# A Mamba-2 scan followed by a GELU network: one filler matmul moved in, one pad taken out, and three state decays given to ScalarE

## The chip, the core and the metric

The kernel runs on one core of a Trainium2 chip. The metric is the device time of one execution in microseconds (us); lower is better. A core has five engines that run side by side, each through its own list of instructions in order: TensorE (PE; its weight loads are listed apart as PEld), VectorE (DVE), ScalarE (ACT), GpSimd (POOL) and SyncE (SP, here only for starting transfers). They wait for one another through semaphores. Matmuls write into PSUM, a small memory of eight banks; everything else lies in SBUF.

## What is computed

Two stages, the second on the output of the first. The first is a state-space scan over 4 batches, 8 heads, 768 steps, with values of width 32 and a state of 16 x 32 for each head:

```python
for c in range(nc):                      # chunks of 32 steps
    cum = np.cumsum(log_a[:, :, sl], axis=-1)
    L = np.exp(cum[..., :, None] - cum[..., None, :]) * causal
    CB = np.einsum('bhin,bhjn->bhij', Cc, Bc)
    y_intra = np.einsum('bhij,bhjd->bhid', CB * L, xc)
    y_inter = np.einsum('bhin,bhnd->bhid', Cc, state) * np.exp(cum)[..., None]
    y[:, :, sl] = y_intra + y_inter
    Bx = np.einsum('bhjn,bhjd->bhjnd', Bc, xc) * decay_from_j
    state = decay_full * state + np.sum(Bx, axis=2)
```

The second takes the 3072 rows of 256 values: `h = x @ w_in` (256 x 2048), `g = h * sigmoid(1.702 h)`, `out = g @ w_out` (2048 x 256).

## The kernel before

The 3072 rows are six groups (g = 0 to 5), each of one chunk of 128 steps of all four batches, 512 rows. A group's scan is done in two pairs of batches; `pairs` names the two pairs of a group, PG and PG + 1 being those of group 1. A chunk is cut into two sides of 64 steps.

**Scan of one group.** `score` multiplies C with B (L626) into an area of PSUM, four banks that exist once (the pool `psa`, tag "cb"). `weigh` (L637, VectorE) multiplies the decays L with those scores, one call for each pair. `gain` (L657, TensorE) computes what each side adds to the state. `keep(g, i)` makes the state after side i: `decayed` (L675) multiplies the state before with the decay over the side into a tile "old" (L679, VectorE, one buffer), and two instructions (L696) add the gain. `carry_first` does the same for the second side of group 0: one product L679 and one sum (L997, by `plus`). `finish` has two steps: `inter` (L738) multiplies the states with C, `intra` (L751) multiplies the weighed L with x; both add into the area of PSUM that the scores were in, and ScalarE copies the sums to yT (L785). Group 0 is different: `early` in `intra` means that its sums lie in four banks of their own, that each bank is copied when it is done (L763), and that `dense`, a matmul of ones with ones whose result nobody reads (L440), stands ahead of the products of the first pair. `pads` are the same in small: 32 x 4 outputs (L436).

**The network.** For group 0, `hidden` (L812) multiplies yT with w_in for 16 columns blocks f, ScalarE applies the activation (L816), and `project_all` multiplies with w_out (L910). From group 1 on, products of 2 x 2 blocks are done with seven multiplications instead of eight (L868, L878, L970, and L977 for the last group), from sums that VectorE prepares (`mix_in` L830, `mix_y` and `mix_g` L836, `mix_w` L933).

**The weights** come as 64-bit floats. VectorE and ScalarE put them together as 32-bit floats (L203 to L251), piece by piece, during the start, the hidden layer of group 0 and its projection; `narrow(9)` is the last piece.

**The order** is written out by hand, and `in_order` at the end keeps it on every engine. `at(in_project[0], f, ...)` puts work of group 1's scan into the projection of group 0, ahead of its block f: at 9 the scores, the gains, the states and the weighings, at 13 the first step of `finish` and `mix_in(1)`, at 15 its second step. At the start, one bank area takes the decays of the first pair (masks L522, two `dense`, the pads, then `differ_of` L528, which waits for the cumulative sums of VectorE, L377); the scores of group 0, its `weigh` in halves, `finish(range(PG), (0,))`, `gain`, and `finish(range(PG), (1,))` follow. In the last of these the second pair's products stand for t = 0 first: half k = 0, half k = 1, each of eight matmuls. The trace lists every matmul of 32-bit floats as two records.

Of the kernel before, what the change touches and what calls it, by code (L numbers as in the profile page):

```python
# [11 lines left out]
AF = mybir.ActivationFunctionType  # L12
# [4 lines left out]
P = 128  # L17
# [18 lines left out]
def kernel(  # L36
# [31 lines left out]
    nc = tc.nc  # L68
# [363 lines left out]
    def pads(n, t, start=True):  # L432

        for i in range(n):
            c = 32 * (i % R)
            nc.tensor.matmul(out=t[c:c + 32, :4], lhsT=ones[:32, :32], rhs=ones[:32, :4],  # L436
                             start=start, stop=True, tile_position=(0, c), skip_group_check=True)
# [177 lines left out]
    def score(pairs):  # L615

        cb = area(f"cb{pairs[0]}").rearrange("p r (k e) -> p r k e", k=2 * PG)
        for n, p in enumerate(pairs):
            s = st[p]
            BT, CT = s["BT"], s.pop("CT")  # L620
            s["cb"] = cb[:, :, 2 * n:2 * n + 2]
            for k in range(2):
                for i, side in enumerate(SIDES):
                    for r in range(R):
                        rows = slice(32 * r, 32 * r + 32)
                        nc.tensor.matmul(  # L626
                            out=s["cb"][side, r, k].rearrange("p (q i) -> p q i", q=Q),
                            lhsT=BT[rows, k, side], rhs=CT[rows, k, :, side],
                            start=True, stop=True, tile_position=(32 * r, H * i),
                            skip_group_check=True)  # L630

    def weigh(p, ks=(slice(0, 2),)):

        Lv = Ls[p].rearrange("p k r q i -> p k r (q i)")
        cb = st[p]["cb"].rearrange("p r k e -> p k r e")
        for k in ks:
            nc.vector.tensor_tensor(out=Lv[:, k], in0=Lv[:, k], in1=cb[:, k], op=ALU.mult)  # L637
# [3 lines left out]
    def gain(pairs, sides=range(2)):  # L641

        g = pairs[0] // PG
        sides = [i for i in sides if i == 0 or g < NG - 1]
        for i in sides:
            if g == 0:
                A = area("A0_1")[:, 0] if i else begun_y["banks"][2][:, 2 * P:]
            else:
                A = bank(f"A{g}_{i}")
            increment[g, i] = A[:, :NB * Q * D].rearrange("p (b e) -> p b e", e=Q * D)  # L650
        for p in pairs:
            b = place(p)[1]
            for k in range(2):
                for r in range(R):
                    heads = slice(Q * r, Q * r + Q)
                    for i in sides:
                        nc.tensor.matmul(  # L657
                            out=increment[g, i][32 * r:32 * r + 32, b + k],
                            lhsT=BE[p][0][SIDES[i], k, r],
                            rhs=rx[p][SIDES[i], k, heads].rearrange("p h d -> p (h d)"),  # L660
                            start=True, stop=True, tile_position=(H * i, 32 * r),
                            skip_group_check=True)
# [12 lines left out]
    def decayed(g, i):  # L675

        t = ssd.tile([P, NB, Q * D], FP32, tag="old", name=f"old{g}_{i}", bufs=1)
        e = i * H + H - 1
        nc.vector.tensor_tensor(out=t, in0=state[g][:, 0] if i else state[g - 1][:, 1],  # L679
                                in1=since[g][:, :, e:e + 1].to_broadcast([P, NB, Q * D]),  # L680
                                op=ALU.mult)
        return t
# [17 lines left out]
    def keep_both(g):  # L700
        for i in range(2):
            keep(g, i)

    def finish(pairs, steps=range(2)):


        g, first = divmod(pairs[0], PG)
        early = pairs[0] < PG
        if 0 in steps:
            if early:  # L710
                banks = begun_y["banks"] = [bank(f"y0_{i}") for i in range(4)]
                y = [t[:, :2 * P].rearrange("p (k i) -> p k i", i=H) for t in banks]
                begun_y[0] = [[y[2 * t + i] for t in range(NK)] for i in range(2)], set()
            else:
                both = area(f"y{pairs[0]}")[:, :, :len(pairs) * 2 * H].rearrange(
                    "p (s t) (k i) -> p s t k i", s=2, i=H)
                begun_y[pairs[0]] = [[both[:, i, t] for t in range(NK)] for i in range(2)] + [both], set()
        y, begun = begun_y[pairs[0]]

        def begin(i, t, parts):  # L720
            new = not begun & {(i, t, q) for q in parts}
            begun.update((i, t, q) for q in parts)
            return new

        def inter(n, p, ts=range(2)):

            b = place(p)[1]
            for k in range(2):
                for i in range(2):
                    if g == 0 and i == 0:  # L730
                        continue
                    old = (state[g][:, 0] if i else state[g - 1][:, 1])[:, b + k]
                    for r in range(R):
                        t = r // 2
                        if t not in ts:
                            continue
                        rows, to = slice(32 * r, 32 * r + 32), Q * D * (r % 2)
                        nc.tensor.matmul(  # L738
                            out=y[i][t][to:to + Q * D, 2 * n + k], lhsT=old[rows],
                            rhs=st[p]["CsT"][rows, k, SIDES[i]],  # L740
                            start=begin(i, t, range(Q * (r % 2), Q * (r % 2) + Q)), stop=early,
                            tile_position=(32 * r, to), skip_group_check=True)

        def intra(n, p, ts=range(2)):
            L = Ls[p]
            for k, t in [(k, t) for t in ts for k in range(2)] if early else [
                    (k, t) for k in range(2) for t in ts]:
                for q in range(HB):
                    h = t * HB + q
                    for i, side in enumerate(SIDES):  # L750
                        nc.tensor.matmul(  # L751
                            out=y[i][t][D * q:D * q + D, 2 * n + k], lhsT=rx[p][side, k, h],
                            rhs=L[side, k, h // Q, h % Q],
                            start=begin(i, t, (q,)), stop=not early, tile_position=(H * i, D * q),
                            skip_group_check=True)

        cols = slice(2 * first * P, 2 * (first + len(pairs)) * P)

        if first == 0 and g not in yT:
            yT[g] = ffn.tile([P, NK, TG], FP32, tag="yT", name=f"yT{g}")  # L760
        if early:
            def copied(i, t):
                nc.scalar.activation(  # L763
                    yT[g][:, t, cols].rearrange("p (k s i) -> p s k i", s=2, i=H)[:, i], y[i][t],
                    AF.Copy)

            if 0 in steps:
                for t in range(NK):
                    dense(begun_y["banks"][0][:, 2 * P:])
                    intra(0, pairs[0], (t,))  # L770
                return
            for t in range(NK):
                intra(1, pairs[1], (t,))
                copied(0, t)
                for n, p in enumerate(pairs):
                    inter(n, p, (t,))
                copied(1, t)
        else:
            for step in steps:
                for n, p in enumerate(pairs):  # L780
                    (inter, intra)[step](n, p)
            if 1 not in steps:
                return
            for i in range(2):
                nc.scalar.activation(  # L785
                    yT[g][:, :, cols].rearrange("p t (k s i) -> p s t k i", s=2, i=H)[:, i], y[2][:, i],
                    AF.Copy)
        state.pop(g - 1, None)
        for p in pairs:
            st.pop(p)  # L790
            Ls.pop(p)
# [292 lines left out]
        mask_banks(1, r, seconds[r])  # L1084
    for k in range(2):
        dense(both[:, k, 2 * P:], 4 - k, False)
    pads(17, both[:, 0, 2 * P:], False)
    differ_of(0)
    turn_blocks(0, "C")
    turn_blocks(0, "B")  # L1090
# [66 lines left out]
    def at(places, i, *work):  # L1157
        places.setdefault(i, []).extend(work)
# [12 lines left out]
    for i, k, c in ((2, 1, 1), (3, 2, 2), (4, 4, 4), (5, 6, 8), (6, 9, 12), (7, 12, 15)):  # L1171
# [12 lines left out]
       lambda: ends_turned(PG + 1), lambda: mask_blocks(PG), lambda: mask_blocks(PG + 1),  # L1184
       lambda: clip_rows(1), lambda: decay_rows(1), lambda: since_start(PG, nc.gpsimd),
       lambda: since_start(PG + 1, nc.gpsimd), lambda: narrow(9))
    at(in_project[0], 9, lambda: score(pairs), lambda: gain(pairs), carry_first, lambda: keep_both(1),
       lambda: weigh(PG), lambda: weigh(PG + 1))
    at(in_project[0], 13, lambda: finish(pairs, (0,)))
    at(in_project[0], 15, lambda: finish(pairs, (1,)))  # L1190
    at(in_project[0], 13, lambda: mix_in(1),
# [198 lines left out]
```

## Time and profile before

| what | value |
|---|---|
| median of 3 runs | 349.52 us (349.3 to 349.52) |
| the profiled execution, its own time | 349.2 us |
| its span, first to last instruction | 347.5 us |
| granted TensorE clock | 1.000 |
| DMA | 25.79 MB, mean 74 GB/s |

Every number of the trace below is in us from the start of the span. "Busy" counts an engine's instructions; matmuls overlap in the array, so a record of 0.38 us may be followed by the next 0.22 us later. A text in square brackets, `[0.93 <-DVE L L637]`, gives how long the engine stood idle before the instruction and what released it; "issue" stands for idle time in which the engine waited for nothing that the profile shows. "x16" counts records. Where one line has many forms, times are of one form only.

The page cuts the span into 40 slices of 8.7 us; a digit is a busy share in tenths:

```profile
PE   7999999989999999999999999999999999999996
DVE  7899999999799897839985639985555653555463
ACT  6689664005454324644333543442444322554320
PEclk9999999999999999999999999999999999999999
```

VectorE is as busy as TensorE in the first ten slices, where it puts the weights together and scans, and half idle after the middle. ScalarE stands still in the eighth and ninth slice, during the end of the projection of group 0.

### The profile page before, as it was taken

To read this page: it belongs to the slowest core of one execution; us is meant where nothing else is said; L and a number is where in the kernel's file an instruction comes from. 1 tells how busy PE (TensorE), PEld (TensorE's weight loads), DVE (VectorE), ACT (ScalarE), POOL (GpSimd) and SP (SyncE) were. 2 spreads that over 40 slices of the span, in tenths; PEclk is the share of its full clock that TensorE was granted. 3 is DMA by queue.
4 is the path that set the end of the run, shared out by engine and by line. 5 is a ranking of instruction groups with operands and counts; after the bars stand their busy time and mean duration, and the time that the engine had idled before them with its cause. 6 is when DMAs were issued, how large, how long until landed. Compare 5 with 4: busy or idle time off the path is not lost.

```text
span 347.5 us, 8555 instructions
## 1 busy us (share of the span) xinstructions
PE 340.7 (98%) x3514; PEld 281.0 (81%) x3514; DVE 257.6 (74%) x489; ACT 149.6 (43%) x335; POOL 41.5 (12%) x80
## 2 busy tenths in 40 slices
PE   7999999989999999999999999999999999999996
PEld 5669964545788888888888888888888888899996
DVE  7899999999799897839985639985555653555463
ACT  6689664005454324644333543442444322554320
POOL 8306500300495000000000000000000000000000
PEclk9999999999999999999999999999999999999999
DMA  4799974703638000554122326120000120000221
GB/s 102 226 299 309 273 154 121 131 9 73 109 90 130 2 0 17 92 110 91 29 35 61 47 87 113 24 32 8 2 4 0 20 32 12 0 2 1 32 31 60
DMA packets 82831, 25.79 MB, mean 74 GB/s; under 512 B 68856, under 2 KB 81144, under 8 KB 82792
## 3 DMA queue, kind: packets, MB, share of 16 engines
q1 hardware_dynamic: 79912, 23.19, 31.1%
q0 software_dynamic: 1888, 1.74, 2.3%
q8 instruction: 27, 0.44, 0.6%
q10 hardware_dynamic: 992, 0.33, 0.4%
q14 instruction: 12, 0.10, 0.1%
HBM read 21.99 MB, written 3.24 MB: 73 GB/s over the span
## 4 chain that ended last, share of the span: by engine, by line
PE 80%; DVE 14%; issue 2%; ACT 2%; ACTq 1%; POOL 0%; DVEq 0%
PE acc L970 28%; PE X L868 19%; PE Y L878 14%; PE acc L977 7%; DVE p L245 3%; PE y L751 2%; PE h L812 2%; PE y L738 2%; PE o L910 2%; DVE m L231 2%; DVE p L203 1%; PE cb L626 1%; DVE m L206 1%; DVE w_in L251 1%; DVE L L637 1%
## 5 line engine op out<-in xcount | busy, mean ns | idle before, releaser
L873 ACT ACTIVATE ac<-X 128x256 f32<-128x256 f32 x76 | 29.1, 383 | 79.7 <-PE X L868 79.3
L970 PE MATMUL acc<-mg,mw 128*128 128x256 f32 x192 | 54.5, 379 | 0.0
L997 DVE TENSOR_TENSOR gT<-Y,ac 128x512 f32<-128x512 f32 x38 | 26.2, 690 | 37.0 <-PE Y L878 33.6
L845 ACT ACTIVATE gT<-gT 128x512 f32<-128x512 f32 (+1 forms) x76 | 39.3, 519 | 31.7 <-DVE gT L997 31.0
L868 PE MATMUL X<-my,mi 128*128 128x256 f32 x152 | 45.1, 379 | 0.0
L997 DVE TENSOR_TENSOR gT<-Y,b 128x256 f32<-128x256 f32 x38 | 15.8, 419 | 34.4 <-PE Y L878 34.4
L970 PEld LDWEIGHTS acc<-mg,mw 128*128 128x128 f32 x192 | 36.5, 190 | 5.0
L812 PE MATMUL h<-yT,w_in 128*128 128x128 f32 (+2 forms) x206 | 36.2, 335 | 0.0
L970 PE MATMUL acc<-gT,w_out 128*128 128x256 f32 x128 | 35.5, 379 | 0.0
L812 PEld LDWEIGHTS h<-yT,w_in 128*128 128x128 f32 x206 | 27.8, 191 | 7.4 <-issue 5.6
L868 PEld LDWEIGHTS X<-my,mi 128*128 128x128 f32 x152 | 28.0, 190 | 3.8
L910 PE MATMUL o<-gT,w_out 128*128 128x512 f32 x64 | 28.6, 597 | 0.0
L836 DVE TENSOR_TENSOR mg<-gT 128x512 f32<-128x512 f32 x40 | 27.2, 681 | 0.0
L970 PEld LDWEIGHTS acc<-gT,w_out 128*128 128x128 f32 x128 | 24.2, 190 | 3.4 <-ACT yT L785 0.2
L873 ACT ACTIVATE b<-X 128x256 f32<-128x256 f32 x38 | 14.6, 384 | 20.6 <-PE X L868 20.2
L868 PE MATMUL X<-yT,w_in 128*128 128x256 f32 x76 | 23.2, 389 | 0.0
L878 PE MATMUL Y<-yT,w_in 128*128 128x256 f32 x76 | 22.7, 381 | 0.0
L878 PE MATMUL Y<-my,mi 128*128 128x256 f32 x76 | 22.6, 379 | 0.0
L868 PE MATMUL X<-my,w_in 128*128 128x256 f32 x76 | 22.6, 381 | 0.0
L878 PE MATMUL Y<-yT,mi 128*128 128x256 f32 x76 | 22.4, 379 | 0.0
L910 PEld LDWEIGHTS o<-gT,w_out 128*128 128x128 f32 x64 | 11.8, 190 | 13.2 <-issue 12.7
L1029 POOL DMA_DIRECT2D out_dram<-ob x32 | 17.3, 550 | 26.3 <-DVE ob L1024 26.1
(146 smaller groups left out, 574.5 us busy)
## 6 DMA issues: line engine op xcount, KB each, us to landing
a<-scratch SPq DMA_DIRECT2D x18, 256.0 KB
bits<-in_moe_w_out_dram SPq DMA_DIRECT2D x8, 512.0 KB
x<-in_x_dram SPq DMA_DIRECT2D x20, 128.0 KB
bits<-in_moe_w_in_dram SPq DMA_DIRECT2D x8, 256.0 KB
bits<-in_moe_w_in_dram SPq DMA_DIRECT2D x4, 512.0 KB
out_dram<-ob SPq DMA_DIRECT2D x128, 16.0 KB
af<-in_a_dram SPq DMA_DIRECT2D x20, 64.0 KB
zC<-in_C_dram SPq DMA_DIRECT2D x36, 32.0 KB
```

The source lines that it names most:

```text
L245: nc.vector.scalar_tensor_tensor(out=p2[:, cols], in0=low[:, cols], scalar=0x80000000, in1=p2[:, cols], op0=ALU.bitwise_and, op1=ALU.bitwi ...
L812: nc.tensor.matmul(out=h[:, cols], lhsT=w_in[:, f, k], rhs=yT[g][:, k, cols], start=(k == 0 and e == 0), stop=(k == NK - 1), skip_group_ch ...
L836: nc.vector.tensor_tensor(out=t[:, 0:2], in0=B[:, :, 1], in1=B[:, 0], op=ALU.subtract)
L845: nc.scalar.activation(o, i, AF.Silu, scale=GELU_SCALE)
L868: nc.tensor.matmul(out=s["X"], lhsT=lhsT, rhs=rhs, start=i == "1", stop=i == "4", skip_group_check=True)
L873: nc.scalar.activation(copy, s["X"], AF.Copy)
L878: nc.tensor.matmul(out=o, lhsT=lhsT, rhs=rhs, start=s.pop("new", False), stop=i != "5", skip_group_check=True)
L910: nc.tensor.matmul(out=o[c], lhsT=w_out[:, c, f], rhs=gT[g, f // 2][:, f % 2], start=(f == 0), stop=(f == NF - 1), skip_group_check=True)
L970: nc.tensor.matmul(out=acc[g][0][i], lhsT=w, rhs=h, start=(j == 0 and (i, 0) in begins), stop=(j == NF // 2 - 1), skip_group_check=True)
L977: nc.tensor.matmul(out=o[k] if type(o) is list else o[:, cols], lhsT=h[:, cols], rhs=w, start=(j == 0 and (i, k) in begins), stop=(j == NF ...
L997: nc.vector.tensor_tensor(out=o, in0=v, in1=w, op=ALU.add)
L1029: (nc.sync if g else nc.gpsimd).dma_start(out=rows[:, b, :, cols], in_=t[32 * r:32 * r + 32, b * P:(b + 1) * P].rearrange("p (u e) -> p u ...
```

## The change

Three things. `decayed` does the product for g below 2 on ScalarE, as four copies with a scale, one for each batch (128 x 64 each), instead of one instruction of VectorE (128 x 256). `keep_both(1)`, which stood ahead of both weighings of group 1, becomes two calls, one after each weighing. In `intra` of group 0, for the second pair and t = 0, one `dense` is put between its halves k = 0 and k = 1, and the pads at the start become 16 instead of 17.

```diff
@@ decayed
         t = ssd.tile([P, NB, Q * D], FP32, tag="old", name=f"old{g}_{i}", bufs=1)
         e = i * H + H - 1
+        if g < 2:
+            for b in range(NB):
+                nc.scalar.activation(t[:, b], (state[g][:, 0] if i else state[g - 1][:, 1])[:, b],
+                                     AF.Copy, scale=since[g][:, b, e:e + 1])
+            return t
         nc.vector.tensor_tensor(out=t, in0=state[g][:, 0] if i else state[g - 1][:, 1],
                                 in1=since[g][:, :, e:e + 1].to_broadcast([P, NB, Q * D]),
                                 op=ALU.mult)
@@ intra
             for k, t in [(k, t) for t in ts for k in range(2)] if early else [
                     (k, t) for k in range(2) for t in ts]:
+                if early and n and not t and k:
+                    dense(begun_y["banks"][0][:, 2 * P:])
                 for q in range(HB):
@@ the start
     for k in range(2):
         dense(both[:, k, 2 * P:], 4 - k, False)
-    pads(17, both[:, 0, 2 * P:], False)
+    pads(16, both[:, 0, 2 * P:], False)
     differ_of(0)
@@ the order within the projection of group 0
-    at(in_project[0], 9, lambda: score(pairs), lambda: gain(pairs), carry_first, lambda: keep_both(1),
-       lambda: weigh(PG), lambda: weigh(PG + 1))
+    at(in_project[0], 9, lambda: score(pairs), lambda: gain(pairs), carry_first, lambda: weigh(PG),
+       lambda: keep(1, 0), lambda: weigh(PG + 1), lambda: keep(1, 1))
```

## The prediction

> **What bounds the kernel now.** I read the busy shares first, then who waited for whom on TensorE, then the order of time around the longest wait, then the same at the second place that the change touches.
>
> ```profile
> PE 340.7 (98%) x3514; PEld 281.0 (81%) x3514; DVE 257.6 (74%) x489; ACT 149.6 (43%) x335; POOL 41.5 (12%) x80
> ...
> PE ab L528 <- DVE cum L377: 1.0, 1, 1.0
> PE y L738 <- DVE L L637: 0.9, 1, 0.9
> PE busy L447 <- PEq L1374: 0.9, 1, 0.9
> PE y L751 <- issue: 0.5, 1, 0.5
> ```
>
> TensorE is busy 98% of the span, and its whole list of waits has four entries, 3.3 us together. Whoever removes one of them, without adding TensorE work, moves everything behind it; whoever shortens work on another engine anywhere else gains nothing. Two of the four, y L738 and y L751, lie where the change works. In order of time the first is this:
>
> ```profile
> 64.02 7.13 PE L910 MATMUL o<-gT,w_out 128*128 128x512 f32 x16
> 66.45 0.41 DVE L679 TENSOR_TENSOR old<-S,L 128x256 f32<-128x256 f32 x1
> 66.90 0.42 DVE L997 TENSOR_TENSOR S<-S,old 128x256 f32<-128x256 f32 x1
> 67.36 0.42 DVE L679 TENSOR_TENSOR old<-S,since 128x256 f32<-128x256 f32 x1
> 67.90 0.61 DVE L696 SCALAR_TENSOR_TENSOR S<-A,part,old 128x128 f32<-128x128 f32 x2
> 68.55 0.42 DVE L679 TENSOR_TENSOR old<-S,since 128x256 f32<-128x256 f32 x1
> 69.07 0.61 DVE L696 SCALAR_TENSOR_TENSOR S<-A,part,old 128x128 f32<-128x128 f32 x2
> 69.60 2.34 DVE L637 TENSOR_TENSOR L<-L,cb 128x1024 f32<-128x1024 f32 x2
> 72.09 1.29 PE L738 MATMUL y<-CsT,S 32*64 32x64 f32 x64 [0.93 <-DVE L L637]
> 76.94 1.48 PE L751 MATMUL y<-L,x 64*32 64x64 f32 x128
> 78.46 1.09 ACT L785 ACTIVATE yT<-y 128x512 f32<-128x512 f32 x2 [20.54 <-PE y L751]
> ```
>
> Columns: start, length, engine, line, operation, count. VectorE goes through eight steps without a pause (carry_first, keep, keep, weigh, weigh), and TensorE, done with the projection at 71.15, stands until the second weighing ends at 71.94: finish writes its sums into the PSUM area that the weighings read. ScalarE has nothing from 57.92 to 78.46. At the other place, early in the kernel:
>
> ```profile
> 11.78 0.70 PE L440 MATMUL y<-ones 128*128 128x256 f32 x2
> 12.41 0.45 PE L751 MATMUL y<-L,x 64*32 64x64 f32 x32
> ...
> 13.60 0.17 PEld L751 LDWEIGHTS y<-L,x 64*32 64x32 f32 x10 [0.25 <-DVE bits L170]
> 14.44 0.31 PE L751 MATMUL y<-L,x 64*32 64x64 f32 x7 [0.52 <-issue]
> ```
>
> The weight loads of the first half of the second rows (k = 0) end at 13.35; the second half starts at 13.60, after its weighing ended at 13.55, does nine records, and pauses from 13.92 to 14.44 for nothing that the profile names, before the last seven.
>
> **The change, part by part.** *(a) States.* VectorE loses the three old products (L679), and one keep moves behind the second weighing. What is left ahead of finish, with start-to-start times of the rows above: the sum of carry_first 0.46 (66.90 to 67.36), a weighing 1.13 (half of 69.60 to 71.86), one keep of two instructions 0.65 (67.90 to 68.55), the last weighing 1.22 (the median of L637). From 66.45, where the weight join before it lets go, that ends at 66.45 + 0.46 + 1.13 + 0.65 + 1.22 = 69.91; with the 0.15 between the end of the weighing (71.94) and TensorE's start (72.09), TensorE could go at 70.06.
>
> *(b) ScalarE* gets three groups of four copies, 128x64 each, a shape that the trace doesn't have. Nearest rows: the copies of L396 (128x128) come 0.29 apart, those of L603 (128x256) 0.40 apart with a mean of 0.494. From 0.29 and 0.40 the line goes to 0.24 at 64 columns; above, 0.494 each with no overlap. I take 0.25, since fewer columns must lie at the low end. Group one, for carry_first, has its inputs (S0, the first group's decays) long before, and runs in ScalarE's gap from 57.92. Group two needs the sum of carry_first, which ends at 66.87: four copies end at 67.87 (by 0.25) or 68.85 (by 0.494). VectorE comes for them at 66.45 + 0.46 + 1.13 = 68.04, so it waits 0 to 0.81, and finish may go at 70.06 to 70.87. Group three uses the same buffer as group two: it waits for the keep that reads it (about 68.7), ends about 69.7 (70.7 by the high price), and the last keep follows the second weighing. Behind it on VectorE stand mix_in and the transposes, at about 70.5 instead of 71.86. Queued behind the copies on ScalarE is only L785 at 78.46.
>
> *(c) What TensorE gets.* Its work ahead of finish is unchanged: it arrives when its own queue lets it. Where it doesn't stall, the next matmul starts 0.07 before the modelled end of the one before (76.94 against 77.01 for L751), so 71.08. Both ends of (b) lie before that. L738 starts at 71.08 instead of 72.09: **1.01 us gained**, for 0.93 by the list of waits alone. Where L738 doesn't stall (91.41) its 64 records take 1.16 and not 1.29, so up to 0.13 more; I leave that to the range. Only 1.01 of VectorE's 2.03 (72.09 - 70.06) counts.
>
> *(d) Where the stall could go next.* Behind it TensorE has no wait to the end, and VectorE runs ahead: y copies end 0.6 before hidden at 80.17, the second group's weighings at 89.15 against L738 at 91.41. All these are released by TensorE or by VectorE, which come forward by 1.01 and about 1.3. The loads that meet them: x for the next gain, issued at 77.83 when L751 frees its buffer, moves along, and with a landing of at most 4.2 (this tensor's loads through POOL) is there at 82.0 for a gain at 83.70; the spread for the scan at 79.75 was issued from 66.35, and no transfer is busy from 70 to 72. I cost it at nothing.
>
> *(e) Filler and pad.* The filler is one full matmul, two records, like L440 at 11.78: 0.63 until the next L751 starts. It stands between k = 0 and k = 1, so it can begin at 13.35 and delays k = 1 from 13.60 to 13.98, or at the worst, begun only at 13.60, to 14.23. Nine records later (0.17 of weight loads) come 14.15 to 14.40, still inside the pause that ends at 14.44. I cost it at 0: its cover is 0.25 of waiting for VectorE and 0.52 of pause. If the pause is not tied to the clock but to the instruction, it moves along, and the filler costs 0.38, at most 0.63, straight on the path into hidden (16.28). The pad: 34 records in 0.47, so 0.03 less, ahead of a wait of 1.00 for VectorE (6.00): nothing.
>
> The trace's instruction queue q8 moved 27 packets, 0.44 MB, one of them at 11.6, another at 16.9, none from 13.8 to 14.6. The Trainium skill (Runtime: NRT & Kernel Launch, Instruction fetch mechanics) says that an engine's program is streamed in 16 KiB blocks of 256 instructions, fetched ahead, and that crossing a block is mostly hidden; 0.44 MB in 27 packets agrees with the size, and by that rule a pad less and a filler more leave every block boundary behind the filler at the same instruction, so the pause stays before the same seven records. By the words "mostly hidden" the pause would be no crossing at all, and the sum is the same.
>
> *Sum:* -1.01 + 0 + 0 = -1.01 on a profiled execution of 349.2 (span 347.5, and 1.7 around it), which is 0.32 under the median of 349.52. Taken off the median: **348.5**.
>
> **The rivals.**
>
> 1. *The filler is not hidden.* For it: a full matmul holds off the small ones (0.63 at 11.78), and nothing names what ends the pause. Against: the pause lies right behind it and is longer than 0.38. Time: 349.52 - 1.01 + 0.38 = 348.9, to 349.1 with 0.63.
>
> 2. *ScalarE becomes the last.* It decides when the four copies take more than 71.08 - 0.15 - 1.22 - 0.65 - 66.87 = 2.19, or 0.55 each. At 0.7 each finish goes at 66.87 + 2.8 + 0.65 + 1.22 + 0.15 = 71.69, a gain of 0.40: 349.1. Against: copies of four times the size (L603) have a mean of 0.494.
>
> 3. *The microsecond is given back* at a later wait (a load with a fixed time of issue): 349.5. Against: (d).
>
> 4. *Slower: the clock.* The pads stand in TensorE's 1.00 of idling before 6.00. If one fewer let the granted clock fall there, the decay products L528, 2.63 on the chain of waits from 6.00 to 8.63, would take up to twice as long: 349.52 - 1.01 + 2.63 = 351.1; it decides from 1.01 of loss on. Against: the granted clock is 1.000, every slice has a 9, and the pad is 0.03 of work.
>
> The Trainium skill (TensorE: Matmul & The Clock Gate, Part 1: The HAM clock gate) says that the clock halves after an idle window of about 3.4 us that runs free of the kernel, not after short gaps. The 1.00 us gap at full clock agrees; by that rule 4 costs nothing.
>
> **How the numbers follow.** A measurement of this kernel can tell about 0.2%, 0.70 us, from no change: faster means under 348.82. The forecast, 0.60, with its own range 348.2 (the 0.13 more and the spread of 0.2 between runs) to 348.8. Rival 1: 0.20, of which 0.06 falls under 348.82. Rival 2: 0.05. Rival 3: 0.07, of which 0.02 ends over 350.2. Rival 4: 0.08. Faster 0.66, within 0.23 (0.14 + 0.05 + 0.05, rounded down), slower 0.11 (0.02 + 0.08, rounded up). The range goes from 348.2 to 349.5: it takes in both ends of rivals 1 and 2 and leaves out rival 4, half of rival 3 and the forecast's tail.
>
> **What would show it.** In the profile after: y L738 gone from TensorE's waits and starting near 71.1; no L679 on VectorE between 66 and 71, and its second weighing ended near 69.9; four copies in 1.0 on ScalarE between the weighings; L751's pause still ending near 14.4 and L812 starting near 16.3; behind that the same rows 1.0 earlier to the end. Wrong would be: L812 later than 16.6 (rival 1), a wait of L738 for VectorE that waits for ScalarE (2), a new TensorE wait after 80 (3), L528 longer than 2.7 (4).

## The result and the profile after

The changed kernel takes 348.21 us (median of 7, 348.04 to 348.78) against 349.6 (median of 7, 349.3 to 350.49) before: a ratio of 0.9962, 95% interval 0.995 to 0.9974, so 0.9 to 1.7 us less. The profiled execution after takes 348.21, its span is 346.5: against the profiled one of before (349.2, span 347.5) 1.0 less. In some executions of both kernels the granted TensorE clock falls for some microseconds and the time grows by 0.5 to 5.3, so "at full clock" below means the median of the executions with a mean clock of at least 0.997.

The busy shares after, from the page:

```profile
PE 341.3 (98%) x3514; PEld 281.2 (81%) x3514; DVE 256.3 (74%) x486; ACT 152.4 (44%) x347; POOL 42.1 (12%) x80
```

TensorE's whole list of waits, after (columns: engine and line, releaser, us in total, times, longest):

```profile
PE ab L528 <- DVE cum L377: 0.9, 1, 0.9
PE busy L447 <- PEq L1381: 0.9, 1, 0.9
PE y L758 <- DVE bits L170: 0.2, 1, 0.2
```

The wait of the states' matmul (L738 before, L743 now) is gone, and so is the pause "issue" of L751 (L758 now). VectorE lost 1.3 us of work, ScalarE gained 2.8. In order of time, the stretch in which the wait was:

```profile
62.27 1.21 PE L626 MATMUL cb<-CT,Bt 32*64 32x128 f32 x64
...
64.19 7.13 PE L917 MATMUL o<-gT,w_out 128*128 128x512 f32 x16
...
66.69 0.41 DVE L1004 TENSOR_TENSOR S<-S,old 128x256 f32<-128x256 f32 x1
...
67.02 1.21 DVE L637 TENSOR_TENSOR L<-L,cb 128x1024 f32<-128x1024 f32 x1
67.13 1.07 ACT L681 ACTIVATE old<-S,since 128x64 f32<-128x64 f32 x4 [8.03 <-DVE S L1004]
68.23 0.61 DVE L701 SCALAR_TENSOR_TENSOR S<-A,part,old 128x128 f32<-128x128 f32 x2
68.76 1.21 DVE L637 TENSOR_TENSOR L<-L,cb 128x1024 f32<-128x1024 f32 x1
68.94 1.06 ACT L681 ACTIVATE old<-S,since 128x64 f32<-128x64 f32 x4 [0.74 <-DVE S L701]
70.03 0.61 DVE L701 SCALAR_TENSOR_TENSOR S<-A,part,old 128x128 f32<-128x128 f32 x2
...
71.26 1.16 PE L743 MATMUL y<-CsT,S 32*64 32x64 f32 x64
```

The four copies on ScalarE run exactly under the first weighing: they end at 68.20, the weighing at 68.23. The second weighing ends at 69.97, 1.29 before TensorE comes. TensorE now goes from the projection into the states' matmul without a stop.

Cut in three, the 1.0 of the profiles is: from the start to the scores of group 1 (L626) 0.17 more (62.10 before, 62.27 after); from there to the states' matmul 1.00 less (9.99 and 8.99); from there to the end, with spans given to 0.1, about 0.2 less (275.4 and 275.2), of which 0.13 is that matmul itself, 1.16 instead of 1.29. Behind it TensorE waits for nothing, as before.

The other place, around the filler:

```profile
13.28 0.35 PE L758 MATMUL y<-L,x 64*32 64x64 f32 x16
13.56 0.70 PE L440 MATMUL y<-ones 128*128 128x256 f32 x2
14.19 0.34 PE L758 MATMUL y<-L,x 64*32 64x64 f32 x16
...
16.06 4.15 PE L819 MATMUL h<-yT,w_in 128*128 128x512 f32 x9
```

The filler takes 0.63 until the next L758. All sixteen records of the second half follow in one piece, and hidden starts at 16.06 instead of 16.28. Yet L626 comes 0.17 later than before: what TensorE gained at the start it lost again in the hidden layer, whose second part starts at 25.84 instead of 25.67. VectorE was late there, because the first piece of the weights was:

```profile
12.34 0.29 DVE L203 TENSOR_SCALAR p<-bits 128x256 uint32<-128x256 uint32 x1 [0.25 <-DMA bits<-in_moe_w_in_dram]
```

Before, this instruction ran at 12.06 with no wait. The lateness goes on through the weights: the join for the fourth block of w_in starts at 20.93 instead of 20.71.

### The profile page after: what moved, and what is told of

Its sections match the earlier page's. It is cut to its first block, busy times and chain, and to the rows that moved or that the text cites. A ratio compares the mean times of both kernels' runs of the same rounds, so it can differ in the third digit from the quotient of the medians.

```text
span 346.5 us, 8565 instructions
## 1 busy us (share of the span) xinstructions
PE 341.3 (98%) x3514; PEld 281.2 (81%) x3514; DVE 256.3 (74%) x486; ACT 152.4 (44%) x347; POOL 42.1 (12%) x80
## 4 chain that ended last, share of the span: by engine, by line
PE 97%; ACT 1%; ACTq 1%; DVE 1%; issue 0%; DVEq 0%
PE acc L977 28%; PE X L875 19%; PE Y L885 14%; PE h L819 10%; PE o L917 8%; PE acc L984 7%; PE y L758 3%; PE cb L626 2%; PE y L743 2%; PE A L657 1%; PE ab L528 1%; ACTq L130 1%; ACT L322 0%; PE y L440 0%; ACT cum L373 0%
## 5 line engine op out<-in xcount | busy, mean ns | idle before, releaser
L411 DVE TENSOR_TENSOR_SCAN L<-a,idents 128x1024 f32<-128x1024 f32 x9 | 20.5, 2273 | 0.0
```

What stands on the lines that cost most here:

```text
L411: nc.vector.tensor_tensor_scan(out=L, data0=ra[p].rearrange("p k e -> p (k e)"), data1=idents.rearrange("p h i -> p (h i)"), initial=0.0, ...
```

## The experiments

Each kernel was timed beside the kernel before; ratios go with 95% intervals. Falls of the clock make these times scatter more than the first ones; the mean clock of an execution shows them (0.985 to 0.995 instead of 1.000). The kernel before has 349.75, 349.46, 349.84 and 349.59 at full clock in the four sets of runs.

**1. The states' part alone** (`states_only`, again as `states_only_again`). Against the changed kernel:

```diff
-                if early and n and not t and k:
-                    dense(begun_y["banks"][0][:, 2 * P:])
...
-    pads(16, both[:, 0, 2 * P:], False)
+    pads(17, both[:, 0, 2 * P:], False)
```

> The states' part alone: decays on ScalarE and the keeps between the weighings, with 17 pads and no filler, so the start is that of the kernel before. Theory A (all of the gain is the wait of TensorE ahead of finish): L738's wait of 0.93 is gone, its second weighing ends near 69.9, time 1.0 under before, as the whole change has it within 0.3. Theory B (the filler also gains, by closing the pause of 0.52 in L751): the pause between the two halves' records is back, and the time lies 0.3 to 0.5 over that of the whole change, so 0.9 to 1.0 under before where the whole change has 1.4.

Measured: ratio 0.9969 (0.9933 to 1.0006), and 0.9949 (0.9914 to 0.9985) the second time; at full clock 348.43 and 348.63, so 1.3 and 1.2 under before. The states' matmul starts at 71.20 with no wait. The pause of 0.55 in L751 was there in the first profile and missing in the second, which is the same program. So the whole gain is in the states' part, and one and the same program runs with the pause or without it.

**2. The filler and the pad alone** (`filler_only`, again as `filler_only_again`): states and order as before, the rest of the change in. Against the kernel before:

```diff
+                if early and n and not t and k:
+                    dense(begun_y["banks"][0][:, 2 * P:])
...
-    pads(17, both[:, 0, 2 * P:], False)
+    pads(16, both[:, 0, 2 * P:], False)
```

> The filler and 16 pads alone; states and order as before. Theory A: same time as before within 0.2; the wait of L738 for VectorE stays at 0.9 or more. Theory B in its plain form (an earlier hidden layer is an earlier end): 0.2 to 0.5 faster. B in its weak form: hidden starts 0.2 to 0.5 earlier but the wait ahead of finish grows by as much, since VectorE sets it, and the time is that of before.

Measured: 1.0004 (0.9971 to 1.0037) and 0.9997 (0.996 to 1.0034); at full clock 349.99 and 349.56. No gain. The profile of the first happened to hold a long pause and a fall of the clock. TensorE there:

```profile
13.78 0.70 PE L440 MATMUL y<-ones 128*128 128x256 f32 x2
14.41 0.32 PE L753 MATMUL y<-L,x 64*32 64x64 f32 x9
15.50 0.31 PE L753 MATMUL y<-L,x 64*32 64x64 f32 x7 [0.77 <-issue]
```

With the filler in place the pause is back, 0.77 long, and again ahead of the last seven records. By stretches (from:to, length, then busy us with counts for PE, PEld, DVE, ACT and POOL, granted clock, DMA share, GB/s):

```profile
12.00:16.00 4.00, 3.02 (x108) 1.89 (x108) 3.35 (x12) 1.68 (x5) 1.17 (x4) 1.00 0.80 242
16.00:20.00 4.00, 4.00 (x66) 2.58 (x61) 3.06 (x10) 2.68 (x7) 0.00 (x0) 0.52 0.83 247
20.00:24.00 4.00, 4.00 (x7) 1.73 (x6) 3.29 (x10) 3.81 (x7) 0.00 (x0) 0.63 1.00 335
```

After the stretch in which TensorE is busy for 3.02 of 4 us, the clock is at half from 16.1 to 22.9. L626 starts at 66.34 there instead of 62.1. In this execution the wait for VectorE ahead of the states' matmul is missing although the order is the old one: TensorE is 4.2 late, so VectorE is done in time.

**3. The order alone** (`order_only`): all products on VectorE as before, only the line of the order changed.

```diff
-    at(in_project[0], 9, lambda: score(pairs), lambda: gain(pairs), carry_first, lambda: keep_both(1),
-       lambda: weigh(PG), lambda: weigh(PG + 1))
+    at(in_project[0], 9, lambda: score(pairs), lambda: gain(pairs), carry_first, lambda: weigh(PG),
+       lambda: keep(1, 0), lambda: weigh(PG + 1), lambda: keep(1, 1))
```

> Only the order within the projection: weigh, keep, weigh, keep, with all three old products still on VectorE; 17 pads, no filler. If VectorE's steps ahead of finish are what counts, the chain is 0.46 + 0.46 + 1.13 + 0.54 + 0.65 + 1.22 from 66.45, which ends at 70.91, and with 0.15 finish can start at 71.06, when TensorE arrives: the whole gain of 1.0 without ScalarE, 348.6. If ScalarE's part is needed, the wait stays at 0.5 or more and the gain is under 0.5.

Measured: 0.9939 (0.9908 to 0.997), at full clock 348.37. VectorE, and TensorE's matmul behind it:

```profile
67.53 1.21 DVE L637 TENSOR_TENSOR L<-L,cb 128x1024 f32<-128x1024 f32 x1
68.66 0.42 DVE L679 TENSOR_TENSOR old<-S,since 128x256 f32<-128x256 f32 x1
69.19 0.61 DVE L696 SCALAR_TENSOR_TENSOR S<-A,part,old 128x128 f32<-128x128 f32 x2
69.72 1.21 DVE L637 TENSOR_TENSOR L<-L,cb 128x1024 f32<-128x1024 f32 x1
```

```profile
71.20 1.16 PE L738 MATMUL y<-CsT,S 32*64 32x64 f32 x64
```

The second weighing ends at 70.93, just ahead of TensorE. One line has the whole gain; ScalarE's part is not needed for it.

**4. ScalarE alone** (`scalar_only`): the copies in, the old order, 17 pads, no filler. Against the kernel before:

```diff
+        if g < 2:
+            for b in range(NB):
+                nc.scalar.activation(t[:, b], (state[g][:, 0] if i else state[g - 1][:, 1])[:, b],
+                                     AF.Copy, scale=since[g][:, b, e:e + 1])
+            return t
```

> Only the decays on ScalarE; both keeps stay ahead of both weighings; 17 pads, no filler. If ScalarE's copies stand on the path when no weighing covers them: the sum ends at 66.87, four copies 1.07 to 67.97, keep to 68.60, four copies from 68.70 to 69.77, keep to 70.41, weighings to 72.67, finish at 72.82, so the wait is 1.7 instead of 0.9 and the time 0.7 over before, 350.3. If fewer VectorE instructions are what counts, the chain is 1.25 shorter and the gain 1.0.

Measured: 1.0002 (0.9968 to 1.0036), at full clock 350.16, 0.4 over before. Nothing covers the copies, and VectorE waits for them twice:

```profile
66.93 0.41 DVE L1002 TENSOR_TENSOR S<-S,old 128x256 f32<-128x256 f32 x1
67.37 1.06 ACT L681 ACTIVATE old<-S,since 128x64 f32<-128x64 f32 x4 [8.02 <-DVE S L1002]
68.47 0.61 DVE L701 SCALAR_TENSOR_TENSOR S<-A,part,old 128x128 f32<-128x128 f32 x2 [1.13 <-ACT old L681]
69.18 1.06 ACT L681 ACTIVATE old<-S,since 128x64 f32<-128x64 f32 x4 [0.74 <-DVE S L701]
70.27 0.61 DVE L701 SCALAR_TENSOR_TENSOR S<-A,part,old 128x128 f32<-128x128 f32 x2 [1.19 <-ACT old L681]
70.80 2.34 DVE L637 TENSOR_TENSOR L<-L,cb 128x1024 f32<-128x1024 f32 x2
73.29 1.54 PE L743 MATMUL y<-CsT,S 32*64 32x64 f32 x64 [1.97 <-DVE L L637]
```

VectorE has fewer instructions than before and is later. After TensorE's wait of 1.97 the clock falls here too: this profile shows 0.57 granted from 74 to 78, and four of the twelve executions have a mean of 0.995.

**5. The change without ScalarE's part** (`order_filler`): `decayed` as before, everything else as changed. Against the changed kernel:

```diff
-        if g < 2:
-            for b in range(NB):
-                nc.scalar.activation(t[:, b], (state[g][:, 0] if i else state[g - 1][:, 1])[:, b],
-                                     AF.Copy, scale=since[g][:, b, e:e + 1])
-            return t
```

> The whole change without ScalarE's part: all three old products back on VectorE, the new order, the filler and 16 pads. If the order is what gains: VectorE's second weighing ends near 71.0 instead of 70.0, finish starts at most 0.1 later, time within 0.2 of the whole change. If ScalarE's part is needed: a wait of L738 of 0.3 or more and 0.3 to 0.9 slower than the whole change.

Measured: 0.9965 (0.9942 to 0.9988), at full clock 348.56; no wait ahead of the states' matmul. Beside the whole change in the same set (348.36) it is 0.2 more, within what these runs scatter.

**6. Two fillers and 15 pads** (`two_fillers`).

```diff
                     dense(begun_y["banks"][0][:, 2 * P:])
+                    dense(begun_y["banks"][0][:, 2 * P:])
...
-    pads(16, both[:, 0, 2 * P:], False)
+    pads(15, both[:, 0, 2 * P:], False)
```

> The whole change with two dense matmuls between the halves instead of one, and 15 pads. Theory H (what TensorE does before the hidden layer is covered, because the weights that VectorE puts together hold the first blocks of hidden): the two fillers push L743 and the start of hidden by 0.4 to 0.6 against the whole change, but L626 of group 1 still starts near 62.3, time within 0.2 of the whole change. Theory P (the start is on the path): 0.4 to 0.6 slower than the whole change.

Measured: 0.9944 (0.9908 to 0.9979), at full clock 348.74, 0.4 over the whole change of the same set. Its profile says otherwise: span 346.9 for both, hidden from 16.40 (whole change 16.32), L626 at 62.61 (62.63). Whether a second filler costs is not settled; that one doesn't is (experiments 1 and 8).

**7. 17 pads with the filler** (`no_pad_cut`).

```diff
-    pads(16, both[:, 0, 2 * P:], False)
+    pads(17, both[:, 0, 2 * P:], False)
```

> The whole change, but with 17 pads. If the pad only keeps the place of the instructions behind the filler: a pause of TensorE, where there is one, comes two records earlier in L751 (before the last nine, not the last seven), and the time is that of the whole change within 0.2. If the pad's time counts: 0.03 slower, which nothing here can tell.

Measured: 0.9946 (0.9913 to 0.9979), at full clock 348.31, the same as with 16. Its profile holds no pause, so where a pause would fall wasn't seen. It holds something else: the third piece of weights landed late, VectorE waited 1.5 for it, TensorE 1.0 for VectorE (within hidden, before 19.01), and the span is 347.7. This is one way in which executions at full clock come to differ by a microsecond.

**8. The whole change again** (`whole_again`, `whole_third`).

> The whole change, run once more beside the kernels below. Executions whose mean granted clock is 0.998 or more: median 348.2 to 348.7, 1.0 to 1.4 under before. Theory K (the filler keeps the clock up): none or one of some 12 executions under a clock of 0.995, where before and the variants had about one in four (8 of 35, 3 of 12, 3 of 12, 4 of 12). Theory N (it does not): about one in four here too, since the filler alone had 3 of 12.

> The whole change once more, for the count of executions with a mean granted clock under 0.995 (so far 1 of 18 for the change itself, 2 of 52 for it and its variants with the filler, but 5 of 24 for the filler with the old order). Theory K (the filler makes falls rarer): at most 1 of some 12. Theory N (the start is the same as that of the filler alone, so falls must be as frequent): 2 or 3 of 12. At full clock 348.2 to 348.7.

Measured: 0.996 (0.9935 to 0.9986) and 0.993 (0.9896 to 0.9965); at full clock 348.36 and 348.23, against 349.46 and 349.59 before: 1.1 and 1.4 less. The clock fell in 1 of 11 and in 2 of 13.

**9. No full matmul at all in finish of group 0** (`no_dense`).

```diff
-                if early and n and not t and k:
-                    dense(begun_y["banks"][0][:, 2 * P:])
...
-                    dense(begun_y["banks"][0][:, 2 * P:])
                     intra(0, pairs[0], (t,))
-    pads(16, both[:, 0, 2 * P:], False)
+    pads(19, both[:, 0, 2 * P:], False)
```

> The whole change without any dense matmul in finish of group 0: neither the filler nor the two that stood there before, and 19 pads, so that the place of the instructions behind stays. Theory K (a thinly filled TensorE between 10 and 16 us lets the granted clock fall, and full matmuls between the small ones hinder it): clearly more than one in four of some 12 executions under a clock of 0.995, each 3 to 5 over the others. Theory N (the falls have nothing to do with these fillers): about as many as the whole change has, 1 of 18 so far. Those at full clock within 0.3 of the whole change in both.

Measured: 1.0044 (1.0014 to 1.0073), and the mean clock is 0.994 or less in all twelve executions. By stretches, as above:

```profile
12.00:16.00 4.00, 2.27 (x112) 1.58 (x112) 3.93 (x13) 1.53 (x4) 1.01 (x4) 1.00 0.73 209
16.00:20.00 4.00, 4.00 (x73) 2.55 (x68) 3.83 (x14) 3.37 (x7) 0.00 (x0) 0.70 0.79 245
20.00:24.00 4.00, 4.00 (x10) 1.76 (x9) 3.34 (x10) 3.77 (x8) 0.00 (x0) 0.87 0.90 281
```

In the one profile without a dense matmul TensorE is busy for 2.27 of 4 us, and the clock fell in every execution of this kernel. With the two dense of before, 3.40 in its profile, it falls sometimes; in the changed kernel's profile TensorE is busy for 4.00. Over all kept profiles, the four with a fall ahead of 24 us have 2.27 to 3.08 in this stretch from 12 to 16, the ten others 3.32 to 4.00. But how full TensorE is does not decide alone. The profile of `no_pad_cut`, with its wait of 1.04 in the hidden layer, has this stretch, at full clock before and behind:

```profile
16.00:20.00 4.00, 2.96 (x10) 1.20 (x8) 2.44 (x8) 2.23 (x4) 0.00 (x0) 1.00 0.93 278
```

That is less than the 3.02 after which the clock fell in experiment 2. The pause is a rival: the four profiles with that fall (`filler_only`, its second run, `whole_third`, `no_dense`) have a pause of 0.77 to 1.75 in L751's line just ahead of it, and of the ten others eight have none and two one of 0.52 and 0.55. No run separates the two. What the third dense matmul, the filler, adds is less clear still. The remaining counts:

> The states' part alone (no filler, 17 pads), run once more for the count. Theory K: about one in four of the executions under a clock of 0.995, as in the first run (3 of 12). Theory N: as few as with the filler. At full clock 1.0 to 1.4 under before.

> The filler and 16 pads alone, run once more for the count. Theory K: at most 2 of some 12 executions under a clock of 0.995, and the 3 of 12 of the first run were chance. Theory N: 3 or more again, as many as before has. At full clock within 0.3 of before.

| clock fell in | with the filler | without it |
|---|---|---|
| whole change, three sets | 3 of 31 | |
| two_fillers, no_pad_cut, order_filler | 1 of 34 | |
| filler_only, twice | 5 of 24 | |
| states_only twice, order_only | | 8 of 36 |
| before, four later sets | | 27 of 116 |
| before, the first 7 | | 0 of 7 |
| together | 9 of 89, 10% | 35 of 159, 22% |

(A fall is a mean clock under 0.997. `no_dense` is left out, since it lacks all three dense matmuls, and `scalar_only`, since the fall in its profile lies at 74.) The sum leans to theory K, by which the filler makes falls rarer, but `filler_only` has the same code up to the projection as the whole change and falls as often as before. Whether the filler makes falls rarer stays open.

## Why the prediction was right

The time forecast was 348.5, the gain 1.01; measured are 348.21 and, between the medians, 1.39, between the two profiles 1.0. The mechanism and its price are those that were forecast; the time itself lies only 0.01 above the low end of the range, and the part of it beyond 1.0 has no shown cause (see *The size*).

*(a) VectorE's chain.* Forecast from the release of the weight join to the end of the second weighing: 0.46 + 1.13 + 0.65 + 1.22 = 3.46. Measured: 66.69 to 69.97, 3.28. The weighing doesn't depend on the sum ahead of it and starts 0.33 after it, not 0.46. The first weighing took 1.21 instead of 1.13 and the keep 0.53 instead of 0.65 until the next start, which nearly cancel; the last weighing is as costed (1.21).

*(b) ScalarE's copies.* Forecast about 1.0 for four, by 0.25 each; measured 1.05 to 1.07. The extrapolation from 256 and 128 columns to 64 held, and the high end of 0.494 each was far off. VectorE waited for none of them, but with 0.03 to spare (68.20 against 68.23) and not the 0.17 of the forecast; 1.29 was left behind it, so a small miss would have cost nothing. What the forecast left out: with the old product still on VectorE the chain would have ended in time too, which experiment 3 shows. The price of that product (0.42) was in the rows.

*(c) The gain at the wait.* Forecast: the states' matmul unstalled, 1.01, and up to 0.13 more because it runs in 1.16. Measured between L626 and it: 1.00, and the 0.13 came too (1.16). The starting time is 71.26 and not 71.08, since TensorE was 0.17 late from the start on.

*(d) Where the stall goes.* Nowhere: there is no wait of TensorE after 16 us in the profile after, and the distance from the states' matmul to the end shrank by about 0.2, of which 0.13 is that matmul itself.

*(e) The filler.* Its 0.63 was right, and so was its cost of nothing, but not by the cover that was forecast; that part was luck. The pause that was to hide it does not end at 14.4 in every execution: it is absent from the profile after, 0.77 in experiment 2, 1.75 in the second run of it. What covers the filler is a hold in the hidden layer, by all signs for the weights: hidden starts at 15.94 in `order_only`, without filler and pause, at 16.06 after and at 16.28 before, its weight loads then stand for 0.66, 0.58 and 0.24 until 17.75, 17.80 and 17.68 (the second piece of weights is joined from 17.26 to 17.68 after), and L626 starts at 62.22, 62.27 and 62.10. For the same reason the opening of the prediction, that whoever removes one wait moves everything behind it, does not hold for the pause.

In six profiles that have the pause, with and without the filler, it stands before the same seven records, with one instruction packet of queue q8 at 11.5 and 11.6 where it is 0.5 long and at 13.0 to 14.5 where it is 0.8 to 1.75 long, and it ends 2.2 to 3.0 after that packet. In the eight profiles without a pause the packet is at 11.1 to 11.7. For the place, that agrees with the rule on 16 KiB blocks in the Trainium skill (Runtime: NRT & Kernel Launch, Instruction fetch mechanics); but all six profiles are of programs with the same number of instructions ahead of these records, so they can't tell a block's border from these matmuls themselves. Its "mostly hidden" agrees with the profile after, which has 27 such packets and no pause; where this packet came at 13.0 or later, TensorE stood for 0.77 to 1.75. That the block is what it waits for is inferred from place and time, no run moved the packet by itself.

*The rivals.* 1, the filler not hidden, is refuted for one filler (348.43 and 348.63 without it, 348.21 to 348.36 with it). 2, ScalarE the last, did not happen in this order; its mechanism is real in the other order (experiment 4), at 0.4 over before. 3 did not happen. 4 put the clock at the pad, where nothing happened: 16 or 17 pads give the same. But the clock does fall in this kernel, one step later, at 16 to 24, and costs more than the 2.63 of the rival: executions of the whole change with a fall take 353.3 to 353.5, 5 over the others. The argument against it, that every slice of the profile has a 9, was an argument from one execution. Its rule from the Trainium skill (TensorE: Matmul & The Clock Gate, Part 1: The HAM clock gate), that the clock falls after an idle window of about 3.4 us, does not agree with these runs: in the profile of experiment 9 TensorE stood for at most 0.9 in one piece, and was busy for 2.27 of 4 us, before the clock fell. The measurement decides.

*The size.* Between the medians the gain is 0.4 more than in the profiles. The scatter is part of it (1.1 to 1.4 in the two later sets of the whole change at full clock). Another part may be that VectorE now has 1.29 to spare ahead of the states' matmul where it had none, so that late weights don't reach TensorE twice. No run shows that, and `order_only` speaks against it: it has 0.27 to spare (70.93 against 71.20) and gains 1.38 at full clock (348.37 against 349.75). The cause of these 0.4 stays open.

## What to carry to other kernels

Before giving an engine's work to another, look whether the work has to stand ahead of the wait at all: here, moving one step behind the instruction that others wait for had the whole gain, and handing work over without moving it gained nothing (0.4 over before at full clock, a wait of 1.97 instead of 0.93). Work handed over must find a cover that the receiver's latency fits under; four small copies took 1.07, one vector instruction 0.42. And one profile at full clock says nothing of how often the clock falls: look at the clock of every execution.

## What was not expected of the hardware

The granted clock can fall without any long idling. In the five profiles with a fall TensorE stood for at most 0.77 to 1.97 in one piece, and was busy for 2.03 to 3.08 of a stretch of 4 us, just before it; yet 2.96 of 4 us left the clock at 1.00 in `no_pad_cut`, so this figure alone is not the rule. A fall is to half the clock and has two lengths here: 3.4 (17.6 to 21.0 in `no_dense`, 74.1 to 77.5 in `scalar_only`) and 6.8 (16.1 to 22.9 in `filler_only`, and as long in its second run and in `whole_third`). An execution with a fall is 0.5 to 5.3 longer than those of its kernel at full clock, in most cases more than 3. Two dense matmuls whose results nobody reads, 0.6 each, go with a clock that stays up in 124 of 159 executions; without any it fell in 12 of 12. And TensorE can pause for up to 1.75 after nine of sixteen records of one line, with a late packet of the instruction queue 2.2 to 3.0 ahead of the pause's end; that the packet is the cause is inferred.
